# Strassen's scheme for the second projection of four chunks, with attention masks and one FFT side moved to TensorE

## The chip, the cores and the metric

One Trainium2 chip, one core. The metric is device time in microseconds (us) of one execution. The engines are TensorE (PE in the rows; its weight loads are PEld), VectorE (DVE), ScalarE (ACT), GpSimd (POOL) and SyncE (SP), whose queue issues nearly all transfers.

## The reference, cut to what matters

```python
def reference(...):
    x = attention(q, k, v)                   # 8 batches x 8 heads x 576 x 64, heads 0-3 local, 4-7 strided mask
    X = np.fft.fft(np.fft.fft(x, axis=1), axis=2)
    u = x + np.real(X)                       # 8 x 576 x 512
    un = (u - mean) / np.sqrt(var + 1e-6)
    return u + np.maximum(un @ w_ch1, 0.0) @ w_ch2   # 512 x 2048, then 2048 x 512
```

The masks keep for each query the 32 last positions, or the earlier positions of the same residue modulo 32. The weights arrive in double precision and are turned into pairs of 16-bit halves on the chip.

## The kernel before, in words

The 4,608 rows of u make 18 **chunks** of 256 tokens, two for each batch and two extra ones ("x") of leftover rows; the last four chunks are the second of batch 6, the second x chunk and both of batch 7. A chunk runs `ups` (first projection, lines 1316 to 1341), `hidden` (ReLU, 1343 to 1351) and `downs` (second projection, 1353 to 1374). Every product is made from 16-bit halves in three passes (`W3`: high by high, high by low, low by high). For each of 8 steps `fp`, `ups` issues 24 matmuls of 256 columns (line 1333) into a `ph` buffer, ACT makes the ReLU twice (1348, 1349), POOL makes the low half (1351), and `downs` issues 12 matmuls of 512 columns (1372) that add up in the `acc` banks through the whole chunk. `finish` (1376 to 1386) adds the sum to u on DVE (1380), once for each 128 tokens, and stores both.

Ahead of the chunks stand, for each batch, attention over four pairs of heads (`att_first` at 649 for batch 0, `att_pair32` at 566 for batches 1 and 2 in single precision, `att_pair` at 407 for the rest) and the transform (`fft_batch`, 889, with `products32`, 1025, for batch 0). In the single-precision pairs TensorE makes scores (`scores32`, 536), and `weigh` (768) lets DVE scale them, add the mask and write SBUF (777), take the maximum of each block (784) and subtract it (786); ACT then makes one exponential of the whole tile. The transform of batch 0 folds rows on DVE and partly on POOL (894), multiplies on TensorE (A at 1043 and 1045, B at 1066 to 1071, where each of the two sides of a row block is a sum of its own), and DVE adds the input (1075). `norm` (1130) normalises u, splits it in halves (1157, 1160) and transposes them by a DMA (1162) into `uT`, which `ups` reads.

The weights come through a chain of their own: load, two ACT passes (1194, 1196), two DVE passes (1200, 1203), a Gram product on TensorE for a bound on the norm (1227), scales, and the split (1268 ACT, 1270 DVE). The first weight matrix is scaled by quarters, the second only when all 16 of its pieces have gone through the Gram product, so no `downs` can start before that.

The order on each engine is written at build time by a list scheduler (`Order`, 192): every piece of work is an `Op` with an engine, an estimated duration, buffers that it gets and puts back, events that it needs and sets, and a bias from the table `P`; the scheduler takes the operation that can start first, the lower bias among those that lie close. On the chip the engines keep that order and wait on semaphores. Where TensorE would idle in the plan while the first Gram sums are open, `rest` (1231) fills it with matmuls of zeros (1235). PSUM holds two `big` buffers of two banks (scores, transposes, attention outputs, transform), two `ph` banks and two `acc` banks.

## Time and profile before

| | us |
|---|---|
| median of 3 runs | 963.96 (963.33 to 967.6) |
| the profiled execution, own time | 964.85 |
| its span, first to last instruction | 963.1 |
| PE busy in the span | 929.1 (96%) |
| DVE, ACT, POOL busy | 575.0, 448.5, 298.6 |
| mean granted TensorE clock | 0.985 of 2.4 GHz |

A busy engine is one with an instruction in flight; a group's busy time is the union of its instructions, so a mean of a pipelined matmul (274 ns) is longer than its share of the busy time (398.2 us over 3,456, or 115 ns). Times in the rows count from the start of the span.

### The profile page before, as it was taken

Reading aid. Unit: us, or ns where it says so; the run is one execution under the profiler, and the core shown is the slowest. Engines: PE = TensorE matmul, PEld = TensorE weight load, DVE = VectorE, ACT = ScalarE, POOL = GpSimd, SP = SyncE. Lnnn points to the kernel's source line nnn. Section 1 sums busy time; section 2 is a strip of 40 time slices with the busy share of each in tenths; the row PEclk is TensorE's granted clock in tenths of the full one; section 3 lists DMA queues with packets and bytes.
Section 4 is the critical chain, followed back from the end, with each engine's and each line's share of the span. In section 5 each row is a group of like instructions: output and inputs, shape, how many; then the busy total and the mean of one; then the engine's idle time right before and its main releaser. Section 6 shows DMA issues by size and latency. Waiting matters only on the chain.

```text
span 963.1 us, 23556 instructions
## 1 busy us (share of the span) xinstructions
PE 929.1 (96%) x9947; PEld 649.8 (67%) x9947; DVE 575.0 (60%) x1086; ACT 448.5 (47%) x867; POOL 298.6 (31%) x288
## 2 busy tenths in 40 slices
...
GB/s 335 285 262 174 195 131 158 97 67 184 138 35 137 153 51 123 47 194 88 148 31 131 145 143 29 149 138 150 17 80 126 36 12 39 45 1 45 1 22 23
DMA packets 133610, 105.08 MB, mean 109 GB/s; under 512 B 103136, under 2 KB 111744, under 8 KB 133504
## 3 DMA queue, kind: packets, MB, share of 16 engines
...
## 4 chain that ended last, share of the span: by engine, by line
PE 88%; DVE 5%; DMA 3%; issue 1%; ACT 1%; POOL 0%; SPq 0%; DVEq 0%; POOLq 0%; ACTq 0%
PE acc L1372 38%; PE ph L1333 38%; PE B L1021 2%; PE s L485 2%; PE A L998 2%; PE o L516 1%; DMA v<-in_v 1%; DVE W L1200 1%; DMA vlx<-in_v 1%; DMA W<-in_w 1%; PE o L523 1%; DVE W L1203 1%; PE B L1070 1%; PE A L1045 1%; DMA q<-in_qk 1%
## 5 line engine op out<-in xcount | busy, mean ns | idle before, releaser
L1333 PE MATMUL ph<-uT,W 128*128 128x256 f16 x3456 | 398.2, 274 | 1.3 <-issue 0.5
L1372 PE MATMUL acc<-W,h 128*128 128x512 f16 x1728 | 387.1, 379 | 0.0
L1333 PEld LDWEIGHTS <-W 128*128 128x128 f16 x3456 | 334.8, 98 | 56.2 <-issue 6.2
L1351 POOL TENSOR_TENSOR h<-hf,h 128x512 f16<-128x512 f32 x144 | 181.3, 1259 | 462.8 <-ACT h L1349 377.9
L1372 PEld LDWEIGHTS <-h 128*128 128x128 f16 x1728 | 166.2, 98 | 186.3 <-issue 1.2
L1348 ACT ACTIVATE hf<-ph 128x512 f32<-128x512 f32 x144 | 85.6, 594 | 311.8 <-PE ph L1333 285.3
L1349 ACT ACTIVATE h<-ph 128x512 f16<-128x512 f32 x144 | 85.1, 591 | 0.0
L1380 DVE SCALAR_TENSOR_TENSOR u<-acc,cout,u 128x512 f32<-128x512 f32 x32 | 23.6, 745 | 95.5 <-PE acc L1372 95.5
L1141 POOL TENSOR_TENSOR rstd<-mv,negh 128x1 f32<-128x1 f32 x36 | 25.6, 713 | 85.3 <-DVE mv L1138 75.4
L1160 DVE TENSOR_TENSOR unp<-un,unp 128x512 f16<-128x512 f32 x34 | 30.1, 884 | 30.5 <-ACT unp L1157 30.4
L1151 DVE TENSOR_SCALAR un<-u,mv,rstd 128x512 f32<-128x512 f32 x30 | 17.5, 584 | 42.4 <-POOL rstd L1141 40.4
L462 DVE SCALAR_TENSOR_TENSOR kt<-qk,sc,kt 128x576 f16<-128x576 f32 (+1 forms) x40 | 35.6, 930 | 11.1 <-ACT kt L447 10.9
L786 DVE TENSOR_TENSOR sm<-sm,mx 128x864 f32<-128x864 f32 (+1 forms) x32 | 34.5, 1077 | 0.6
L1120 ACT ACTIVATE pq<-B,fcm 128x128 f32<-128x128 f32 (+7 forms) x105 | 27.2, 380 | 15.9 <-PE B L1021 8.4
L447 ACT ACTIVATE kt<-qk,sc 128x576 f16<-128x576 f32 (+1 forms) x40 | 29.3, 783 | 10.7 <-DVE sc L403 6.9
L1011 DVE SCALAR_TENSOR_TENSOR AT<-A,AT 128x290 f16<-128x290 f32 (+3 forms) x35 | 15.1, 480 | 27.1 <-ACT AT L1006 27.1
L894 POOL TENSOR_TENSOR FD<-E 128x381 f32<-128x381 f32 x8 | 10.4, 1299 | 61.4 <-DVE E L894 61.4
L784 DVE TENSOR_REDUCE mx<-sm 128x9 f32<-128x864 f32 (+1 forms) x32 | 29.1, 908 | 0.6
L1110 DVE TENSOR_TENSOR rt<-pq 128x257 f32<-128x257 f32 (+1 forms) x42 | 18.8, 488 | 16.9 <-ACT pq L1120 14.9
L497 ACT ACTIVATE sm<-sm 128x864 f32<-128x864 f32 (+1 forms) x20 | 16.2, 812 | 26.2 <-DVE sm L786 26.2
L1157 ACT CAST unp<-un 128x512 f16<-128x512 f32 x34 | 20.9, 615 | 15.4 <-DVE un L1151 9.4
...
## 6 DMA issues: line engine op xcount, KB each, us to landing
...
```

What stands on the lines that cost most here:

```text
L447: A.activation(hi, src, AF.Copy, scale=f)
L462: V.scalar_tensor_tensor(out=lo, in0=src, scalar=f, in1=hi, op0=ALU.mult, op1=ALU.subtract)
L784: V.tensor_reduce(out=mx[:, 0:nb], in_=sm, axis=AX.X, op=ALU.max)
L786: on(o).tensor_tensor(out=sm, in0=sm, in1=mx[:, 0:nb].rearrange("p (g o) -> p g o", o=1).to_broadcast([128, nb, w]), op=ALU.subtract)
L1120: A.activation(dst, ps[0:r, c0:c1], AF.Copy, scale=cm[0:r])
L1141: G.tensor_tensor(out=rstd, in0=mv[:, 1:2], in1=negh, op=ALU.pow)
L1160: on(o).tensor_tensor(out=unp[:, 1], in0=un, in1=unp[:, 0], op=ALU.subtract)
L1333: T.matmul(ph[:, i, :], W1[:, 4 * (f0 // 512) + d, x, f0 % 512 : f0 % 512 + 128], self.uhl[y][:, d, :], start=(n == 0), stop=(n == 11))
L1348: A.activation(hf, ph, AF.Relu, scale=HS)
L1349: A.activation(hh, ph, AF.Relu, scale=HS)
L1351: G.tensor_tensor(out=hl, in0=hf, in1=hh, op=ALU.subtract)
L1372: T.matmul(self.acc[s], (hh, hl)[x][:, i, 128 * s : 128 * s + 128], W2[:, f, y, :], start=(f == 0 and n == 0), stop=(f == 15 and n == 2))
```

## The change

- **Second projection.** When a chunk above number 2 is about to start its first projection in the plan and table 3 of 8 is made by then, it runs `ups7`, `hidden7`, `downs7`, `finish7` in place of the old path; that holds for the last four chunks. Two halves of the 256 tokens, of the hidden features and of the output columns make a 2 by 2 block product, done with 7 block products in place of 8. `hidden7` builds the sums of hidden blocks (four DVE or POOL operations), ACT and POOL or DVE split seven blocks of 128 columns. `downs7` issues for each fp 21 matmuls of 256 columns, three of the chunk's first 21 being 512 wide, into both `big` buffers. `finish7` combines the sums on ACT and DVE.
- **Tables.** `seven` waits until attention of batch 7 is through and the second matrix is split, gives back the attention's SBUF pools and spawns `combos`, which makes four differences of weight blocks for each fp.
- **Masks.** In single-precision pairs `scores32` opens each PSUM bank with one matmul of the identity by the mask in 16 bits (480 columns local, 324 strided), and the scores add to it. `soft32` takes the maximum from PSUM. For batch 0 DVE subtracts it from PSUM; for batches 1 and 2 (`X1`, `X2` = 1) ACT makes one exponential for each block with the maximum as its bias, 9 or 11 in all, reading PSUM.
- **Batch 0.** `cos2`, `sin2` and both `side` steps are fixed to DVE. B makes both sides of a row block in one bank of 512 columns, and DVE adds them in three operations. For chunk 0 `norm` transposes on TensorE, with ACT and DVE making the halves out of PSUM, without the DMA.
- **Small things.** The norm bound of a quarter is one DVE operation in place of three; a table of the transform is split in two loads; pools change sides; every number of `P` that steers the order is new.

```diff
         w, per = (WIN, 5) if local else (GR, NG2)
         off = [(g // per) * 512 + (g % per) * w for g in range(nb)]
+        one = ident.bitcast(BF16).rearrange("p (n t) -> p n t", t=2)[:, :, 1]
+        if local:
+            m = mloc.rearrange("p g w -> p (g w)").bitcast(BF16).rearrange("p (g w t) -> p g w t", g=5, t=2)[:, :, :, 1]
+            masks = m, m[:, 1:2].to_broadcast([128, per, w])
+        else:
+            m = mstr.bitcast(BF16).rearrange("p (o w t) -> p o w t", o=1, t=2)[:, :, 0:w, 1]
+            masks = (m.to_broadcast([128, per, w]),) * 2
                 for h in range(2):
                     hs = slice(64 * h, 64 * h + 64)
-                    T.matmul(ps[rows(local, g, h), off[g] : off[g] + w], qk[hs, st : st + 64], qk[hs, S + st : S + st + w], start=True, stop=True)
+                    T.matmul(ps[rows(local, g, h), off[g] : off[g] + w], qk[hs, st : st + 64], qk[hs, S + st : S + st + w], start=False, stop=g in (per - 1, nb - 1))
         return w, off
...
+    def soft32(nm, ps, local, sm, out, split, note, get, put, room, also, sets=""):
+        nb, per, w = (NQB, 5, WIN) if local else (NG, NG2, GR)
+        yield op("V", (1.15 if local else 0.82) + (0.1 if split else 0.0), put=also, note=f"max {nm}")
+        mx = small.tile([128, 2 * NG2], F32, tag="mx", name=f"my{nm}_{room}")
+        src = ps.rearrange("p (b c) -> p b c", b=2)[:, :, 0 : per * w].rearrange("p b (g w) -> p b g w", w=w)
+        V.tensor_reduce(out=mx[:, 0 : 2 * per].rearrange("p (b g) -> p b g", b=2), in_=src, axis=AX.X, op=ALU.max)
+        if split:
+            V.tensor_scalar(mx[:, 0 : 2 * per], mx[:, 0 : 2 * per], -0.125, None, op0=ALU.mult)
+            yield op("A", 2.7 if local else 2.8, get=get, put=f"{put} {room}", sets=sets, note=f"exp {nm}")
+            for g in range(nb):
+                A.activation(out[:, g], src[:, g // per, g % per], AF.Exp, scale=0.125, bias=mx[:, g : g + 1])
+            return
+        yield op("V", 1.25 if local else 0.82, put=room, note=f"sub {nm}")
+        if local:
+            for b, n in ((0, 5), (1, 4)):
+                m = mx[:, 5 * b : 5 * b + n].rearrange("p (g o) -> p g o", o=1).to_broadcast([128, n, w])
+                V.tensor_tensor(out=sm[:, 5 * b : 5 * b + n], in0=src[:, b, 0:n], in1=m, op=ALU.subtract)
+        else:
+            m = mx.rearrange("p (b g o) -> p b g o", b=2, o=1).to_broadcast([128, 2, per, w])
+            V.tensor_tensor(out=sm.rearrange("p (b g) w -> p b g w", b=2), in0=src, in1=m, op=ALU.subtract)
+        yield op("A", 0.92 if local else 0.7, get=get, put=put, sets=sets, note=f"exp {nm}")
+        A.activation(out, sm[:, 0:nb], AF.Exp, scale=0.125)
...
         def side(c0, c1, nm, sd):
-            o = op("V", 0.75 if c0 else 1.4, need=(f"sin{b}" if c0 else nm) if f32 else nm, sets=f"FH{c0}_{b}" if f32 else "", note=f"SD{c0} {b}", alt=dict(G=(1.5, P["LSD"])))
+            o = op("V", 0.75, need=(f"sin{b}" if c0 else nm) if f32 else nm, sets=f"FH{c0}_{b}" if f32 else "", note=f"SD{c0} {b}", alt=None if f32 else dict(G=(1.5, P["LSD"])))
...
-            ps = psbig(f"B{b}_{t}")
-            for i in range(2):
-                R = ps[:, 512 * i : 512 * i + 257]
-                T.matmul(R, zerb, zero.to_broadcast([128, 257]), start=True, stop=False)
-                for g, (c0, w) in enumerate(GROUPS):
-                    k0, k1, st = cols[g]
-                    tc0 = c0 if i or g < 3 else c0 + 255
-                    T.matmul(R[0:r, k0:k1:st], AT[0:w, g, 128 * t : 128 * t + r], tb[0:w, tc0 : tc0 + w], start=False, stop=False)
-                T.matmul(R, zerb, zero.to_broadcast([128, 257]), start=False, stop=True)
-            spawn(sums(b, t, r, xa, xb, ps[0:r, 0:257], ps[0:r, 512:769], "big"), bias=P["t2"] if t == 2 else None)
+            yield op("T", 2.5, get="big" + (" u" if t < 2 else ""), need=" ".join(f"AT{g}_{b}" for g in range(5)), put="f6" if t == 2 else "", sets="!b1" if t == 1 else "", note=f"B{t} {b}")
+            R = psbig(f"B{b}_{t}")[:, 0:512]
+            T.matmul(R, zerb, zero.to_broadcast([128, 512]), start=True, stop=False)
+            c = 0
+            for g, (c0, w) in enumerate(GROUPS):
+                lhs = AT[0:w, g, 128 * t : 128 * t + r]
+                st, k0 = steps[0][g], steps[1][g]
+                if g == 0:
+                    T.matmul(R[0:r, 0:257:4], lhs, tb[0:w, 0:65], start=False, stop=False)
+                    T.matmul(R[0:r, 260:512:4], lhs, tb[0:w, 65:128], start=False, stop=False)
+                    c = 128
+                else:
+                    o = R[0:r].rearrange("p (i k) -> p i k", i=2)[:, :, k0:256:st]
+                    T.matmul(o, lhs, tb[0:w, c : c + 2 * w].rearrange("p (i k) -> p i k", i=2), start=False, stop=False)
+                    c += 2 * w
+            T.matmul(R, zerb, zero.to_broadcast([128, 512]), start=False, stop=True)
+            spawn(sums32(b, t, r, xa, xb, R[0:r]), bias=P["t2"] if t == 2 else None)
...
+    def sums32(b, t, r, xa, xb, R):
+        for i in range(2):
+            yield op("V", 0.68 if i == 0 else 0.75, put="big" if i else "", need="xk0" if i else "", sets=("", (f"u{b}a0", f"u{b}a1", "")[t])[i], note=f"u{t} {b}")
+            if i == 0:
+                if t < 2:
+                    uu = mp.tile([128, 2, DM], F32, tag="u", name=f"u{b}_{t}", bufs=UB)
+                    dst = [uu[:, 0], uu[:, 1]]
+                else:
+                    dst = [xa[0:33, 2], xb[0:33, 2]]
+                V.tensor_tensor(out=dst[0], in0=R, in1=xa[0:r, t], op=ALU.add)
+            else:
+                V.tensor_tensor(out=dst[1][:, 1:512], in0=R[:, 511:0:-1], in1=xb[0:r, t, 1:512], op=ALU.add)
+                V.tensor_tensor(out=dst[1][:, 0:1], in0=R[:, 0:1], in1=xb[0:r, t, 0:1], op=ALU.add)
+        yield from placed(b, t, dst, xa, xb)
...
@@ -1149,6 +1207,18 @@
         else:
             un = mp.tile([128, 2, 257], F32, tag=tag, name=f"un{nm}", bufs=P["RB"]).rearrange("p a b -> p (a b)")[:, 0:DM]
         V.tensor_scalar(un, u, mv[:, 0:1], rstd, op0=ALU.subtract, op1=ALU.mult)
+        if c == 0:
+            yield op("T", 0.95, get="big", put=tag, note=f"uT {nm}")
+            ps = psbig(f"uT{nm}")[:, 0:512]
+            for d in range(4):
+                T.transpose(ps[:, 128 * d : 128 * d + 128], un[:, 128 * d : 128 * d + 128], ident)
+            ps = ps.rearrange("p (d t) -> p d t", d=4)
+            hi, lo = uT[:, 0:4, 128 * s : 128 * s + 128], uT[:, 4:8, 128 * s : 128 * s + 128]
+            yield op("A", 0.65, note=f"uhi {nm}")
+            A.copy(hi, ps)
+            yield op("V", 0.68, put="big", sets=f"uT{nm}", note=f"ulo {nm}")
+            V.tensor_tensor(out=lo, in0=ps, in1=hi, op=ALU.subtract)
...
+    def seven():
+        yield op("S", 0, need=" ".join([f"xd{B - 1}_{hp}" for hp in range(4)] + [f"w1_{m}" for m in range(8)]), note="seven")
+        early.close()
+        late_["p"] = ctx.enter_context(tc.tile_pool(name="late", bufs=1, side="right", reuse_waits="tile"))
+        S_.room["x"] = [S_.now] * 2
+        S_.room["hq"] = [S_.now] * 2
+        yield op("G", 0.5, sets="t2_z", note="zeros")
+        TT[0] = late_["p"].tile([128, 2, 5, 256], F16, name="T0")
+        G.memset(W2[:, 16, 0, 0:256], 0.0)
+        G.memset(TT[0][:, 0, 4], 0.0)
+        for fp in range(8):
+            spawn(combos(fp), bias=P["T"] + 0.1 * fp)
...
+    def combos(fp):
+        o = op("V", 1.15, get="x x", note=f"tr {fp}", alt=dict(G=(2.6, P["LT"])))
+        yield o
+        R = xt(f"tr{fp}").rearrange("p (k a) c -> p k (a c)", k=2)
+        W = W2[:, 2 * fp : 2 * fp + 2]
+        on(o).tensor_tensor(out=R, in0=W[:, :, 0], in1=W[:, :, 1], op=ALU.add)
+        o = op("V", 1.4, note=f"ts {fp}", alt=dict(G=(2.8, P["LT"])))
+        yield o
+        X = xt(f"ts{fp}").rearrange("p (k a) c -> p k (a c)", k=4)
+        b11, b12, b21, b22 = R[:, 1, 0:256], R[:, 1, 256:512], R[:, 0, 0:256], R[:, 0, 256:512]
+        for k, x, y in ((0, b12, b11), (1, b22, X[:, 0]), (2, b22, b12), (3, b21, X[:, 1])):
+            on(o).tensor_tensor(out=X[:, k], in0=x, in1=y, op=ALU.subtract)
+        yield op("A", 1.0, note=f"thi {fp}")
+        if fp:
+            TT[fp] = late_["p"].tile([128, 2, 4, 256], F16, name=f"T{fp}")
+        A.copy(TT[fp][:, 0, 0:4], X)
+        o = op("V", 1.15, put="x x", sets=f"t2_{fp}", note=f"tlo {fp}", alt=dict(G=(2.6, P["LT"])))
+        yield o
+        on(o).tensor_tensor(out=TT[fp][:, 1, 0:4], in0=X, in1=TT[fp][:, 0, 0:4], op=ALU.subtract)
     HS = 2.0**-14
...
         def ups(self):
             c = self.c
+            self.seven = False
+            if c > 2:
+                yield op("T", 0, need=f"uT{c}_0 uT{c}_1 up{c - 1}", note=f"up {c}")
+                self.seven = S_.events.get(f"t2_{P['TQ']}", 1e9) < S_.now
+            spawn(self.downs7() if self.seven else self.downs(), bias=P["dn"])
+            if self.seven:
+                yield from self.ups7()
+                return
             for fp in range(8):
...
+        def hidden7(self, fp, ph):
+            c = self.c
+            yield op("A", 0.62, get="x", put="ph", note=f"relu {c} {fp}")
+            X = xt(f"x{c}_{fp}")
+            A.activation(X[:, 4:8].rearrange("p k t -> p (k t)"), ph, AF.Relu, scale=HS / 2)
+            o = op("V", 0.85, note=f"hsum {c} {fp}", alt=dict(G=(1.7, P["LX"])))
+            yield o
+            for k, x, y, f in ((0, 7, 5, ALU.add), (1, 0, 6, ALU.subtract), (2, 6, 7, ALU.subtract), (3, 4, 1, ALU.subtract)):
+                on(o).tensor_tensor(out=X[:, k], in0=X[:, x], in1=X[:, y], op=f)
+            yield op("A", 0.9, note=f"hhi {c} {fp}")
+            if fp % 2:
+                h = f6(f"h{c}_{fp}").bitcast(F16)[:, 0:1792].rearrange("p (y k t) -> p y k t", y=2, k=7)
+            else:
+                h = late_["p"].tile([128, 2, 7, 128], F16, tag="hq", name=f"h{c}_{fp}", bufs=2)
+            self.h[fp] = h
+            A.copy(h[:, 0], X[:, 0:7])
+            o = op("G", 2.3, put="x", sets=f"h{c}_{fp}", note=f"hlo {c} {fp}", alt=dict(V=(0.98, P["LH"])))
+            yield o
...
+        def downs7(self):
+            c = self.c
+            for fp in range(8):
+                first, last = fp == 0, fp == 7
+                yield op("T", 2.32, get="big big" if first else "", put="f6" if fp % 2 else "hq", need=f"h{c}_{fp} t2_{fp} t2_z" + (f" down{c - 1}" if first else ""), sets=f"down{c}" if last else "", at=0, note=f"down {c} {fp}", slack=0.3)
+                if first:
+                    self.pa, self.pb = psbig(f"pa{c}"), psbig(f"pb{c}")
+                h, t = self.h.pop(fp), TT[fp]
+                w = lambda k, half: lambda y: W2[:, 2 * fp + k, y, 256 * half : 256 * half + 256]
+                tt = lambda k: lambda y: t[:, y, k]
+                wide = {0: W2[:, 1:17:15, 0, 0:256], 2: W2[:, 0:17:16, 0, 0:256], 4: TT[0][:, 0, 2:5:2]}
+                for k, (ps, q, x, m) in enumerate((
+                    (self.pa, 0, 6, w(1, 0)), (self.pa, 1, 1, tt(1)), (self.pa, 2, 4, w(0, 0)), (self.pa, 3, 0, tt(0)),
+                    (self.pb, 0, 2, tt(2)), (self.pb, 1, 5, tt(3)), (self.pb, 2, 3, w(0, 1)),
+                )):
+                    for n, (y, z) in enumerate(W3):
+                        if first and n == 0 and k in wide:
+                            T.matmul(ps[:, 256 * q : 256 * q + 512].rearrange("p (a t) -> p a t", a=2), h[:, y, x], wide[k], start=True, stop=False)
+                        else:
+                            T.matmul(ps[:, 256 * q : 256 * q + 256], h[:, y, x], m(z), start=first and n == 0 and k == 6, stop=last and n == 2 and (k % 2 == 1 or k == 6))
+            spawn(self.finish7(), bias=P["ev"])
...
+        def finish7(self):
+            c, pa, pb = self.c, self.pa, self.pb
+            e = yield op("A", 1.05, get="x", note=f"ev {c}")
+            ev = xt(f"ev{c}").rearrange("p (k a) t -> p k (a t)", k=4)
+            A.activation(ev, pa.rearrange("p (k t) -> p k t", k=4), AF.Copy, scale=cout2)
+            yield op("V", 1.7, put="big", at=e - 0.9, note=f"fin {c}")
+            stt = lambda out, ps, x: V.scalar_tensor_tensor(out=out, in0=ps, scalar=cout2, in1=x, op0=ALU.mult, op1=ALU.add)
+            add = lambda e, out, x, y: e.tensor_tensor(out=out, in0=x, in1=y, op=ALU.add)
+            stt(self.u[0][:, 256:512], pb[:, 512:768], self.u[0][:, 256:512])
+            stt(self.u[1][:, 0:256], pb[:, 256:512], self.u[1][:, 0:256])
+            add(V, ev[:, 1], ev[:, 1], ev[:, 0])
+            u0 = self.u[0].rearrange("p (k t) -> p k t", k=2)
+            u1 = self.u[1].rearrange("p (k t) -> p k t", k=2)
+            add(V, u0, u0, ev[:, 0:2])
+            yield op("V", 0.4, put="big", note=f"fin7 {c}")
+            stt(ev[:, 1], pb[:, 0:256], ev[:, 1])
+            o = op("V", 1.2, note=f"fin7 {c}", alt=dict(G=(2.4, P["LF"])))
+            yield o
+            add(on(o), u0, u0, ev[:, 2:4])
+            add(on(o), u1, u1, ev[:, 1:2].to_broadcast([128, 2, 256]))
+            o = op("V", 0.35, put="x", note=f"fin7 {c}", alt=dict(G=(0.7, P["LF"])))
+            yield o
+            add(on(o), self.u[1][:, 256:512], self.u[1][:, 256:512], ev[:, 3])
+            yield from self.store()
...
@@ -1449,10 +1661,11 @@
     for b in range(1, B):
         spawn(batch(b), bias=1 + 0.1 * b)
+    S_.room["x"], S_.room["hq"] = [], []
+    spawn(seven(), bias=0)
     for ch in chunks:
         spawn(ch.norm(), bias=P["p0"] if ch.c == 0 else P["p1"] if ch.c == 1 else P["pn"])
         spawn(ch.ups(), bias=P["up"])
```

## Rows read from the trace of the kernel before

**Rows 1.** The page: busy us of each engine, share of the span, instructions.
```profile
PE 929.1 (96%) x9947; PEld 649.8 (67%) x9947; DVE 575.0 (60%) x1086; ACT 448.5 (47%) x867; POOL 298.6 (31%) x288
```
**Rows 2.** The page: chain that ended last, shares of the span.
```profile
PE 88%; DVE 5%; DMA 3%; issue 1%; ACT 1%; POOL 0%; SPq 0%; DVEq 0%; POOLq 0%; ACTq 0%
```
**Rows 3.** Windows: length, PE, PEld, DVE, ACT, POOL busy (instructions), clock, DMA share, GB/s.
```profile
0.00:88.00 88.00, 69.03 (x899) 55.73 (x900) 68.88 (x121) 51.56 (x75) 12.28 (x14) 0.88 0.81 273
88.00:146.00 58.00, 51.82 (x754) 44.30 (x753) 48.87 (x92) 31.90 (x56) 14.98 (x13) 0.95 0.58 163
146.00:192.00 46.00, 45.85 (x470) 28.42 (x470) 34.02 (x56) 22.66 (x39) 14.74 (x14) 1.00 0.42 129
192.00:740.00 548.00, 543.84 (x6290) 374.12 (x6288) 375.17 (x733) 286.90 (x584) 196.45 (x192) 1.00 0.44 107
740.00:797.00 57.00, 57.00 (x440) 39.44 (x439) 27.41 (x53) 20.43 (x50) 22.75 (x21) 1.00 0.18 50
797.00:964.00 167.00, 161.51 (x1105) 107.83 (x1102) 20.65 (x34) 35.08 (x65) 37.44 (x35) 0.99 0.09 25
```
**Rows 4.** Windows, line 1235 alone (zero matmuls): length, PE and PEld busy, clock, DMA.
```profile
0.00:88.00 88.00, 24.85 (x347) 23.65 (x347) 0.88 0.81 273
```
**Rows 5.** Chain in order of time, last chunk: start, length, what.
```profile
942.91 5.24 PE ph L1333 x48
948.15 10.37 PE acc L1372 x48
```
**Rows 6.** Timeline of the end: start, length, engine, line, what.
```profile
958.03 1.63 SPq L1386 DMA_DIRECT2D out<-u  x2
958.55 0.75 DVE L1380 SCALAR_TENSOR_TENSOR u<-acc,cout,u 128x512 f32<-128x512 f32 x1 [0.55 <-PE acc L1372]
```
**Rows 7.** Lines by form, DVE and ACT: prices near the new operations.
```profile
L1075 DVE TENSOR_TENSOR u<-rt,xa 128x257 f32<-128x257 f32 x14 | 5.9, 420 | 0.0
...
L870 ACT COPY xb<-xb0a 128x1024 f32<-128x1024 f32 x1 | 1.0, 1012 | 1.0 <-DVE O L894 1.0
```
**Rows 8.** Lines, DVE, 0 to 146 us: the mask, the subtraction.
```profile
L786 DVE TENSOR_TENSOR sm<-sm,mx 128x864 f32<-128x864 f32 (+1 forms) x8 | 8.0, 1006 | 0.2
...
L777 DVE SCALAR_TENSOR_TENSOR sm<-s,mloc 128x480 f32<-128x480 f32 (+1 forms) x10 | 5.6, 599 | 6.6 <-PE s L544 6.6
...
L777 DVE SCALAR_TENSOR_TENSOR sm<-s,mstr 128x324 f32<-128x324 f32 (+1 forms) x8 | 3.3, 458 | 1.0 <-PE s L544 1.0
```
**Rows 9.** Timeline, DVE: a fold; the split alone and beside POOL.
```profile
34.65 2.48 DVE L1270 SCALAR_TENSOR_TENSOR W<-W,scl,W 128x1024 f16<-128x1024 f32 x2 [1.21 <-ACT W L1268]
...
50.10 0.56 DVE L894 TENSOR_TENSOR FD<-E 128x381 f32<-128x381 f32 x1
50.58 3.97 DVE L1270 SCALAR_TENSOR_TENSOR W<-W,scl,W 128x1024 f16<-128x1024 f32 x2
```
**Rows 10.** Timeline, POOL: the folds of batch 0.
```profile
51.48 1.98 POOL L894 TENSOR_TENSOR FD<-tmp 128x384 f32<-128x384 f32 x1
53.54 2.73 POOL L894 TENSOR_TENSOR E<-FD 128x257 f32<-128x257 f32 x2
```
**Rows 11.** Timeline, PE and SP: first product A, uT's transposes, first `ups`.
```profile
56.33 0.75 PE L1045 MATMUL A<-f32a,E 128*65 128x145 f32 x2 [0.67 <-POOL E L894]
...
80.42 3.50 SPq L1162 DMA_TRANSPOSE uT<-unp  x2
...
87.56 0.61 PE L1227 MATMUL gram<-W 128*128 128x128 bf16 x4 [2.80 <-DVE W L1203]
87.96 6.64 PE L1333 MATMUL ph<-uT,W 128*128 128x256 f16 x48
```
**Rows 12.** Line 1351 (POOL, low half): shortest, median, longest ns; first and last start.
```profile
L1351 POOL TENSOR_TENSOR h<-hf,h x144: 1146/1158/2876, 93.3 to 949.5; 128x512 f16<-128x512 f32 x144
```
**Rows 13.** Line 1120 by form (ACT, one block with a pointer scale).
```profile
L1120 ACT ACTIVATE pq<-B,fcm 128x65 f32<-128x65 f32 x14 | 5.3, 378 | 11.3 <-PE B L1021 7.5 <-DVE rt L1110 3.8
```

152 lines of the change are left out of this document (90 added, 62 removed).

## The prediction

> **What bounds the kernel now.** I read the page's busy line first: TensorE is busy for 96% of the span, no other engine over 60% [rows 1]. The chain of waits says the same: 88% of it is TensorE, 5% VectorE, 3% DMA [rows 2]. An average hides the stages, so the table of stretches comes next [rows 3]. From 192 us on TensorE stands still for 4 us in 605 until the last stretch, whose 5.5 us are the end of the kernel; there only TensorE work counts. Until 88 us it is another picture: TensorE shows 69.0 us busy, but 24.9 of these are matmuls of zeros [rows 4], so with the 19.0 idle ones half of the stretch does nothing for the result, while DVE is busy for 68.9. From 88 to 146 us DVE has 48.9 of 58 and TensorE idles 6.2: this is the second weight matrix being prepared, and the first `downs` waits for its end. So the front is set by DVE and the loads, and all behind 146 us by TensorE.
>
> The last chunk gives the price of both projections [rows 5]: 48 matmuls of 256 columns in 5.24 us, 109.2 ns each; 48 of 512 columns in 10.37 us, 216.0 ns each. A chunk's `downs` is 96 of these, 20.74 us.
>
> **Strassen, TensorE.** A new `downs7` is 8 x 21 = 168 matmuls, of which 3 are 512 wide. Taking the 256-column price from `ups`, which also has one weight load for each matmul, it costs 165 x 0.1092 + 3 x 0.2160 = 18.67 us, 2.07 less than before. Four chunks: **-8.3 us**. Bounds: nothing gained if each block waits for its data; -9.1 if the price were half that of 512 columns (165 x 0.1080 + 0.65 = 18.47, 2.27 a chunk). I take -8.3, since the row is of the same shape.
>
> The rule that speaks against this is in the Trainium skill, "TensorE: Matmul & The Clock Gate", section "Back-to-back issue gap": in a stream of pairs of weight load and matmul it gives about 131 ns for 512 columns and 81 for 128, as weight loads share the spacing. By that rule 96 old matmuls would cost 12.6 us and 168 new ones, at some 98 ns by interpolation (an estimate from that page), 16.4, so each chunk would lose 3.8 and the four 15 us in place of the gain of 8.3. The trace here disagrees with the 131 ns: 216.0 [rows 5].
>
> **Work beside it.** For each fp, ACT makes one ReLU and one copy of 7 x 128 = 896 columns where it made two of 512; by 1.01 us for 1,024 columns [rows 7] that is some 1.5 us of a step of 2.62 + 2.33 = 4.95 us. POOL's low half grows from 1.16 us at 512 columns [rows 12] to 2.03 at 896, and four block sums of 128 columns on DVE are under 4 x 0.42 [rows 7]. All stay below the step. Every hidden step holds one of two new `x` buffers from its ReLU to its low half: 0.6 + 1.0 + 0.9 + 2.0, with hand-overs some 5 us; two buffers carry one step each 2.5 us. The tables cost DVE and POOL 8 times two operations of 1,024 columns and four of 256; by 257 columns in 0.42 us that is 8 x 5 = 40 us, and ACT 8 x 1.0. They are spread over the two stretches behind attention, where DVE has 29.6 of 57 us free before the last four chunks begin at 797 us [rows 3], and POOL takes part. Price: nothing; without that cover the first new chunk would simply take the old path, 2.07 us each. `downs7` takes both `big` buffers, but the transform of batch 7 has ended by then.
>
> **The end.** Now one DVE operation of 0.75 us follows the last matmul, then the store [rows 6]. After the change two 256-column additions wait for the last matmul, then come 256, 512, 256, 512, 512 and 256 columns in turn on DVE, ACT's copy of 1,024 columns (1.01 us) running beside. With 0.42 us for 257 columns [rows 7] and 0.75 for 512 [rows 6], and some tenths off where neighbours overlap (an estimate), this is 5 x 0.37 + 3 x 0.60 = 3.65 us: **+2.9 us**. Bounds: +3.6 without overlap, +5 with an addition on POOL, +2 if sums from PSUM start ahead of the last matmul.
>
> **Masks.** One local pair gets two matmuls of 480 columns, a strided one two of 324: 2 x 0.203 and 2 x 0.138 us by the prices above, 1.36 us for the four pairs of a batch. In batch 0 they fall into a stretch half of which is zeros or idle, in batch 1 into 88 to 146 us: both at nothing, hidden by DVE's chain; 1.4 us each if that cover is gone. Batch 2 runs on the saturated engine: **+1.4 us**. The scores now need mask and identity loaded, some tenths of loading ahead of the first scores, and one more table load goes through SP's queue, behind which the weights wait; both are inside the front's bounds.
>
> **The front.** DVE loses the mask step of eight pairs by 146 us: 5.6 us for ten instructions and 3.3 for eight, of which eight and eight go, 7.8 us [rows 8]. In batch 1 the subtraction goes too, half of 8.0 [rows 8], 4.0; four small scalings come, 0.6. Fixing `cos2`, `sin2` and two sides on DVE adds 2 x 0.56 [rows 9] and 2 x 0.84 [rows 7], 2.8. But POOL then leaves it alone: the split took 3.97 us beside POOL and 2.48 alone [rows 9], -1.5. Sum: 9.9 us less DVE work ahead of the first `downs`. Batch 0's 3.9 us of masks lie in the first 24 us, where loads decide, so 6.0 are left. The same is seen along the chain to the first `ups`: A starts at 56.33 behind POOL's folds of 1.98 and 2.73 us [rows 10, 11]; on DVE, from 50.66 on, the two take 1.4, so A starts 4.2 us earlier. B in one bank saves some, and the transposes of 3.5 us in SP's queue [rows 11] go to TensorE, ACT and DVE. The first `ups` at 87.96 stood behind a Gram product that waited 2.8 us for DVE [rows 11]; the next gate is the second matrix. I take **-6 us**, between 0 (loads or staging buffers of the second matrix decide) and -12 (all 9.9 and a shorter Gram wait). For batches 1 and 2 ACT makes 9 or 11 exponentials in place of one; with 0.38 us for the first of five small ones [rows 13], overlapping, 2.5 to 4 us for each pair, hidden while ACT has 26 of 58 us free. The scores' PSUM buffer is held for that long instead of 1.2 us.
>
> **Sum.** -8.3 + 2.9 + 1.4 - 6.0 = -10.0 us against the profiled execution's own 964.85: 954.9. That execution stands 0.9 us above the median of the three runs, so against these **954.0 us** (-1.0%). This measurement can tell about 0.5%, 4.8 us.
>
> **Rivals.**
> - *The front gives nothing.* The second matrix comes in its 16 loads through staging buffers, at a DMA share of 0.58 [rows 3]; if these set the first `downs`, DVE's gain is idle time. Against: DVE is busy 84% there. 960.0 us, no change that can be told. Chance 0.22.
> - *The front gives double*, as the zero matmuls and idle time leave 44 us to be had before 88 us: 947 us. Chance 0.14.
> - *It does not do what it says*: tables or `big` buffers come so late that two chunks' gain is lost, +4: 958. Chance 0.06; free DVE time speaks against it.
> - *The hidden chain becomes the bound* (the other side). DVE's sums and POOL's low half hinder each other: line 1351's median is 1.16 us, its longest 2.88 [rows 12]. The `x` buffer is held 5 us; this decides from 9.9 us on, twice the step. At 11 us a step takes 5.5 in place of 4.95: 32 steps x 0.55 = +17.6 us, 972 us. Chance 0.08: most executions of the row are at the median. The Trainium skill, "GPSIMD Engine Reference", section "8. Key points", says that POOL shares its SBUF interfaces with VectorE's operations of two SBUF inputs, which the new sums are; the trace agrees [rows 9].
> - *Weight loads show.* A load takes 107.83 / 1,102 = 0.098 us [rows 3]. If it were not hidden behind 256 columns of the new pattern, 168 x 0.207 = 34.8 us replace 20.74: +56 in place of -8.3, 1,018 us. `ups` hides it, so chance 0.02. The page's rule above goes the same way; by its figures the time would be some 978.
>
> **How the numbers follow.** The forecast has 0.48, its own range 949 to 959. Faster: 0.48 + 0.14 + 0.06 = 0.68. Same: 0.22. Slower: 0.08 + 0.02 = 0.10. The range leaves out the slower cases and the far end of the double front: 944 to 964.
>
> **What would show it.** In the changed profile: 21 matmuls in about 2.33 us in the last four chunks and TensorE at 100% there; one DVE train of some 3.7 us after the last matmul; first A near 52 us, first `ups` near 80, first `downs` near 140; no more than 5 us of idle TensorE behind 192 us. The forecast is wrong if `downs7` waits on its hidden blocks, if the first `downs` stays at 146 us, or if TensorE waits for `big` buffers in batches 1 and 2.

## The result, and the profile after

The changed kernel takes **957.15 us** (median of 5 runs, 954.85 to 958.69) where the kernel before took 964.67 beside it (5 runs, 963.33 to 967.8): a ratio of 0.9904 [0.9875, 0.9932]. The forecast was 954.0 with 944 to 964. The profiled execution took 954.85 us, 10.0 less than the profiled one before; the forecast's sum was -10.0. So the number came out, but two of its parts did not, and they cancel.

The page first: busy time by engine, and the chain that ended last (against [rows 1, 2]).

```profile
PE 921.2 (97%) x10190; PEld 675.1 (71%) x10190; DVE 664.0 (70%) x1296; ACT 485.8 (51%) x951; POOL 263.5 (28%) x252
...
PE 88%; DMA 4%; DVE 4%; issue 1%; ACT 1%; SPq 1%; ACTq 0%; DVEq 0%
```

TensorE still sets the time; DVE has 89 us more to do, and its part of the chain is 4%, after 5% before. The table of stretches, cut at the new milestones (first `ups` at 82 us, first `downs` at 134), columns as in [rows 3]:

```profile
0.00:82.00 82.00, 65.58 (x840) 50.56 (x841) 58.73 (x110) 46.66 (x68) 3.73 (x8) 0.91 0.79 273
82.00:134.00 52.00, 51.23 (x760) 44.12 (x759) 44.79 (x86) 41.74 (x98) 15.77 (x13) 0.98 0.67 202
134.00:192.00 58.00, 57.83 (x614) 36.87 (x605) 38.32 (x72) 35.50 (x96) 16.07 (x18) 1.00 0.43 129
192.00:797.00 605.00, 598.03 (x6647) 412.00 (x6645) 441.13 (x838) 313.10 (x627) 225.37 (x210) 0.99 0.41 100
```

Ahead of 134 us TensorE idles 17 us in place of 25 ahead of 146. Behind 192 it idles 7.0 us, where 4.2 stood before and at most 5 were forecast.

To see where each kernel gains and loses I took from each trace the start of the first `ups` (first matmul of `ph`), of the first `downs`, and of the `ups` of chunks 2, 3 and 13 in TensorE's order (the 385th, 577th and 2,497th matmul of `ph`). "Rest" is from chunk 13's start to the end of TensorE's last matmul, and "tail" from there to the end of the span. All in us; the kernels below the second line are the experiments.

| kernel | ups | downs | chunk 2 | chunk 3 | chunk 13 | rest | tail |
|---|---|---|---|---|---|---|---|
| before | 88.0 | 146.1 | 214.6 | 254.9 | 739.05 | 219.46 | 4.6 |
| changed | 81.9 | 134.2 | 208.8 | 248.6 | 734.32 | 211.22 | 7.5 |
| changed_again | 83.7 | 136.1 | 210.1 | 250.0 | 733.14 | 211.22 | 7.5 |
| no_strassen | 83.1 | 135.5 | 209.6 | 248.4 | 732.76 | 219.45 | 4.2 |
| masks_on_dve | 83.7 | 137.4 | 210.3 | 248.1 | 731.75 | 215.58 | 7.5 |
| folds_on_pool | 89.5 | 141.1 | 214.7 | 253.9 | 739.73 | 213.91 | 7.5 |
| gather_held | 83.7 | 134.8 | 210.4 | 249.0 | 731.81 | 211.44 | 8.0 |
| order_alone | 101.4 | 159.8 | 242.3 | 288.8 | 762.46 | 219.46 | 4.6 |
| chunk_2_turned_on_tensore | 82.5 | 134.3 | 205.0 | 242.9 | 725.77 | 211.22 | 7.2 |
| last_chunk_old | 86.6 | 137.8 | 211.9 | 250.7 | 731.35 | 217.64 | 4.5 |
| turned_no_strassen | 85.1 | 137.0 | 207.4 | 245.3 | 726.43 | 219.46 | 3.8 |
| turned_last_old | 82.8 | 133.5 | 204.5 | 242.5 | 723.77 | 213.28 | 4.2 |
| turned_last_old_gather_held | 84.0 | 135.8 | 206.2 | 248.1 | 738.37 | 213.28 | 4.1 |
| chunk_0_by_transfer | 89.8 | 143.0 | 216.7 | 253.9 | 734.58 | 211.22 | 7.5 |

The first two lines are the whole result: 4.7 us of lead at chunk 13, 8.24 less in the rest, 3.0 more in the tail, -10.0 in all.

How far a single line can be trusted, four of them tell: changed, changed_again, no_strassen and last_chunk_old run the same order on TensorE, DVE and ACT up to 700 us, and their first `downs` come at 134.2 to 137.8, their chunk 13 at 731.4 to 734.3. So a start is known to some 3 us. Lengths between two starts repeat better, from the first `downs` to chunk 2 for instance 74.0 to 74.6 in these four, and most readings below are such lengths.

The lead over the kernel before was 11.9 us at the first `downs`. It is half gone by chunk 2; in the other three of the four it is 8.3 to 10.6 and 2.7 to 5.0. The timeline of TensorE ahead of chunk 2, and the second of chunk 2's two transposes in SP's queue, in the changed kernel; then two stretches of it (columns as above):

```profile
203.43 1.26 SPq L1232 DMA_TRANSPOSE uT<-unp  x1
...
208.77 4.45 PE L1455 MATMUL ph<-uT,W 128*128 128x256 f16 x20 [2.06 <-DMA uT<-unp]
```
```profile
204.00:209.00 5.00, 1.84 (x58) 1.11 (x57) 3.91 (x9) 0.94 (x1) 4.06 (x5) 0.83 0.86 221
209.00:216.00 7.00, 7.00 (x43) 5.31 (x42) 2.86 (x5) 1.59 (x3) 1.95 (x5) 0.63 0.95 337
```

TensorE is busy 1.84 of 5 us: it has nothing left but a few scores, waits 2.06 us at the end for chunk 2's transposes, which are used 5.3 us after their issue, and then works at a mean granted clock of 0.63 for 7 us, that is, for most of them at the lower level, 1.2 GHz. The kernel before issued the same transposes at 208.48 and used them at 214.56, 6.1 us later, but there work lay between. Its timeline of TensorE (line 631 is attention's product, 1372 `downs`):

```profile
209.10 1.27 PE L631 MATMUL o<-vlx,pT 96*64 96x65 f32 x36
210.30 0.88 PE L620 MATMUL t<-ident,pbt 128*128 128x128 f32 x6
211.02 2.75 PE L1372 MATMUL acc<-W,h 128*128 128x512 f16 x12
213.70 0.93 PE L563 MATMUL o<-vsx,pT 54*64 54x65 f32 x48
214.56 1.70 PE L1333 MATMUL ph<-uT,W 128*128 128x256 f16 x14
```

### The profile page after: what moved, and what is told of

Same layout as the page of the kernel before. It is cut to its first block, busy times and chain, and to the rows that moved or that the text cites. A ratio compares the mean times of both kernels' runs of the same rounds, so it can differ in the third digit from the quotient of the medians.

```text
span 953.1 us, 24270 instructions
## 1 busy us (share of the span) xinstructions
PE 921.2 (97%) x10190; PEld 675.1 (71%) x10190; DVE 664.0 (70%) x1296; ACT 485.8 (51%) x951; POOL 263.5 (28%) x252
## 4 chain that ended last, share of the span: by engine, by line
PE 88%; DMA 4%; DVE 4%; issue 1%; ACT 1%; SPq 1%; ACTq 0%; DVEq 0%
PE ph L1455 30%; PE acc L1581 30%; PE ph L1472 9%; PE pa L1524 4%; PE pb L1524 3%; PE B L1054 2%; PE s L500 2%; PE A L1031 1%; DMA q<-in_qk 1%; PE o L531 1%; DMA vn<-in_vl 1%; PE s L568 1%; PE o L538 1%; DMA vlx<-in_v 1%; DMA W<-in_w 1%
## 5 line engine op out<-in xcount | busy, mean ns | idle before, releaser
L1581 PE MATMUL acc<-W,h 128*128 128x512 f16 x1344 | 302.6, 379 | 0.0
L1560 POOL TENSOR_TENSOR h<-hf,h 128x512 f16<-128x512 f32 x112 | 149.3, 1333 | 334.6 <-ACT h L1558 262.4
L1581 PEld LDWEIGHTS <-h 128*128 128x128 f16 x1344 | 128.7, 98 | 142.7 <-issue 0.5
L1557 ACT ACTIVATE hf<-ph 128x512 f32<-128x512 f32 x112 | 66.8, 596 | 178.6 <-PE ph L1455 134.6
L1524 PEld LDWEIGHTS <-h 128*128 128x128 f16 x660 | 64.6, 98 | 8.9
L1491 DVE TENSOR_TENSOR x<-x 128x128 f32<-128x128 f32 x128 | 31.5, 287 | 43.3 <-ACT x L1487 42.2
L1501 DVE TENSOR_TENSOR h<-x,h 128x896 f16<-128x896 f32 x32 | 34.9, 1092 | 25.0 <-ACT h L1498 24.9
L1498 ACT CAST h<-x 128x896 f16<-128x896 f32 x32 | 30.0, 939 | 42.1 <-DVE x L1491 40.4
L1487 ACT ACTIVATE x<-ph 128x512 f32<-128x512 f32 x32 | 19.1, 597 | 60.1 <-PE ph L1472 60.1
L1524 PE MATMUL pa<-T,h 128*128 128x256 f16 x192 | 31.4, 273 | 0.0
L1524 PE MATMUL pa<-W,h 128*128 128x256 f16 x184 | 30.5, 273 | 0.0
```

The costliest lines, as they stand in the source:

```text
L1491: on(o).tensor_tensor(out=X[:, k], in0=X[:, x], in1=X[:, y], op=f)
L1498: A.copy(h[:, 0], X[:, 0:7])
L1501: on(o).tensor_tensor(out=h[:, 1], in0=X[:, 0:7], in1=h[:, 0], op=ALU.subtract)
L1524: T.matmul(ps[:, 256 * q : 256 * q + 256], h[:, y, x], m(z), start=first and n == 0 and k == 6, stop=last and n == 2 and (k % 2 == 1 or k ...
L1557: A.activation(hf, ph, AF.Relu, scale=HS)
L1560: G.tensor_tensor(out=hl, in0=hf, in1=hh, op=ALU.subtract)
```

## The experiments

They ran in three sets, each on one chip: the first four below (kernel before: 964.67 us, median of 25 runs, from 959.67 to 973.56), the next four (961.46, 11 runs), the last four (958.85, 24 runs). With that spread, medians of different sets say nothing within 3 us; what is compared is the ratio to the runs of before beside them, and the table above.

**No Strassen.** The scheme is left out with its tables, so all chunks use the old second projection.
```diff
-    spawn(seven(), bias=0)
-                self.seven = S_.events.get(f"t2_{P['TQ']}", 1e9) < S_.now
+                self.seven = False
```


> All 18 chunks take the old second projection and no tables are built; all else, and the order up to the tables, is that of the changed kernel. If the four Strassen chunks give back 2.07 us each on TensorE and cost 2.9 us at the end, as the trace of the changed kernel reads (8.2 less, 3.0 more), this runs some 5 us above the changed kernel: about 962 us, its last matmul 8 us later, 4.65 us from there to the end. Rival: the new hidden chain or the tables already ate the gain elsewhere (DVE work for tables beside the last old chunks); then it runs within 2 us of the changed kernel, about 957.

957.92 us (12 runs, 954.45 to 962.63), 0.9928 [0.9899, 0.9957]. The medians differ by 0.8 us and the ratios by 2.3, less than expected; but the rest is 219.45 against 211.22, and the tail 4.2 against 7.5. By the trace the scheme is worth 8.2 - 3.3 = 4.9 us, and this execution came to chunk 13 1.6 us earlier, which the scheme doesn't explain: changed_again, below, has the scheme and comes there within 0.4 us of it. The times left it open (962 was expected); turned_no_strassen, below, settles it.

**Masks on DVE again.** Order held.
```diff
-            T.matmul(ps[...], one, m, start=True, stop=False)
+            V.scalar_tensor_tensor(out=sm[:, g0:g1], in0=src[...], scalar=1.0, in1=m, op0=ALU.mult, op1=ALU.add)
```


> The masks go back to DVE (the same order of work, one mask step from PSUM to SBUF ahead of each maximum; blocks of exponentials then read SBUF), and the 24 mask matmuls are gone. If DVE sets the front, the first second-projection matmul moves from 134.2 us to about 138 (the 3.9 us of batch 1's four mask steps; batch 0's lie in the shadow of the loads) and the end by 4 less 1.4 of TensorE in batch 2: about 2.5 us slower than the changed kernel, 959.5. Rival: the lead of the front came from the new order alone; then the first such matmul stays at 134 and the kernel is 1 to 3 us faster, about 955.

958.12 us (8 runs), 0.9942 [0.9919, 0.9966]. First `downs` at 137.39, where about 138 was expected. From the first `ups` to the first `downs` it takes 53.7 us, against 51.1 to 52.4 in changed, changed_again, no_strassen, gather_held and last_chunk_old: the masks' place is worth 1.3 us or more there, with TensorE waiting 2.1 us for DVE in the Gram products, where the changed kernel shows none. Chunk 13 starts 1.4 us earlier than in changed_again, not later: batch 2's masks are off TensorE, no wait at chunk 2 is over 0.5 us (several small ones are left), and no lower clock follows. The profiled execution then loses 2.5 us at 749, where TensorE waits for DVE (told at last_chunk_old). So in this execution nothing of the masks' gain is left at chunk 13; the medians leave it open.

**Folds on POOL again** (`cos2`, `sin2` and both sides of batch 0; order held).
```diff
-                tt_(on(o), sd[:, t], FD[:, 0, c0:c1], FD[:, 1, c0:c1], f)
+                tt_(on(o) if b else G, sd[:, t], FD[:, 0, c0:c1], FD[:, 1, c0:c1], f)
```


> The four last folds of batch 0 go back from DVE to POOL, with the order of all engines as in the changed kernel. If these folds are on the way to the first chunk, the first product A starts some 3 us later (POOL took 1.98 and 2.73 us where DVE takes 0.55 and 0.76), the first chunk's first projection by 3, and the first second projection by 1 to 3: end 1 to 3 us later, 958 to 960. Rival: the second weight matrix is the next gate whatever chunk 0 does; then the first second projection stays at 134.2 and the end at 957.

960.48 us (12 runs), 0.9954 [0.9926, 0.9982]. The timeline of POOL and of TensorE:
```profile
56.74 3.36 POOL L927 TENSOR_TENSOR O<-FD 128x255 f32<-128x255 f32 x2
60.06 1.40 POOL L927 TENSOR_TENSOR E<-FD 128x257 f32<-128x257 f32 x2
...
60.83 1.43 PE L1078 MATMUL A<-f32a,E 128*65 128x145 f32 x4 [6.68 <-POOL E L927]
```
In the changed kernel DVE makes them in a fraction, and A starts at 55.01:
```profile
53.87 0.75 DVE L927 TENSOR_TENSOR O<-FD 128x255 f32<-128x255 f32 x2
54.53 0.76 DVE L927 TENSOR_TENSOR E<-FD 128x257 f32<-128x257 f32 x2
...
55.01 0.80 PE L1078 MATMUL A<-f32a,E 128*65 128x145 f32 x4 [1.81 <-DVE E L927]
```
First `ups` and `downs` come 5.8 and 5.0 us later than in changed_again, more than the 3 and the 1 to 3 expected. So the new order leans on DVE's folds. But this is not what they brought against the kernel before, where POOL made them and started them earlier; its first product A on `E` stands only 0.2 us behind the changed kernel's:
```profile
55.19 0.46 PE L1045 MATMUL A<-f32a,E 128*65 128x145 f32 x2 [2.17 <-POOL E L894]
```

**Gather held.** Batch 2's load of its first rows may be ordered only behind chunk 2's transposes, so that it doesn't share the DMA engines with them.
```diff
-... need=" ".join(f"xd{b}_{hp}" for hp in range(4)), note=f"xa {b}")
+... need=" ".join(f"xd{b}_{hp}" for hp in range(4)) + (" uT2_0 uT2_1" if b == 2 else ""), note=f"xa {b}")
```


> In the changed kernel TensorE idles 2.1 us at 206.7 us for the transposed halves of chunk 2, while the loads of batch 2's rows (direct and gathered) fill the DMA engines, and then shows a granted clock of 0.58 for the next stretch of 5 us. Here these loads wait until chunk 2's transposes are through. If the transposes were late because of these transfers, the idle time and the half clock go: 4 to 5 us faster than the changed kernel, about 952.5. Rival: the transposes are late for themselves, or the later loads make batch 2 late instead; then the idle time only moves, and the time stays within 1.5 us of 957.

952.99 us (5 runs), 0.9883 [0.9857, 0.9908], the 952.5 expected, but by luck, not for the reason given. TensorE's wait for the transposes is no shorter:
```profile
203.87 1.26 SPq L1232 DMA_TRANSPOSE uT<-unp  x1
...
206.05 0.39 SPq L912 DMA_DIRECT2D xa<-xd  x1
...
210.42 2.96 PE L1455 MATMUL ph<-uT,W 128*128 128x256 f16 x13 [2.98 <-DMA uT<-unp]
```
The load (912) still goes out before the transposes have landed, 2.2 us behind their issue where it was 1.8 in the changed kernel, so the edit did not part the two; whether the load delays them is not answered. Up to 210 us the order on TensorE, DVE and ACT is the changed kernel's; behind that the edit moved it, and chunk 13 starts 1.3 us earlier than in changed_again. What lowers the time stays open; by the ratios it is 2 us, inside the intervals.

**The changed kernel once more.** No edit.

> The changed kernel once more, with no edit, so that the runs beside it are compared on one chip. Theory: the 2.1 us wait of chunk 2's `ups` for the transposes' transfer at 207 us, and the half clock behind it, belong to the order of the work, so they are there again: over 1.5 us of wait, 3.4 to 6.8 us at the lower clock between 200 and 220 us, and about 957 us. Rival: they were an accident of one execution; then the wait is under 0.5 us and the profiled time about 952.

954.09 us (6 runs), 0.9908 [0.9873, 0.9943]. The wait is there again, 2.83 us, with the lower clock behind it; no_strassen has 2.42 and last_chunk_old 2.90. It belongs to the order.

**The order alone.** The kernel before with the changed kernel's numbers in `P`.

> The kernel before with the new numbers of the order and none of the new code. Theory: the numbers were fitted to other parts and are worth nothing without them: 962 to 972 us, first `downs` no sooner than 143 us, where the changed kernel has 134. Rival: the order alone made the shorter front; then first `ups` stand at about 82 us, first `downs` at about 134 to 138, and the time is 957 to 960 with the Strassen steps' 5.2 us missing.

987.96 us (6 runs), 1.0263 [1.0224, 1.0301]: worse than the theory's 962 to 972. The two longest waits of TensorE (us, times, longest):
```profile
PE gram L1228 <- DVE W L1204: 7.2, 3, 5.1
PE ph L1334 <- DMA uT<-unp: 7.2, 2, 6.8
```
The numbers are a fit to durations that the old code doesn't have: the first `downs` moves to 159.8, and chunk 2's transposes are bare for 6.8 us, with no head start at all. The gain is the new parts' and the order's together, and none of it the order's alone.

**Chunk 2 turned on TensorE**, as chunk 0 is.
```diff
-        if c == 0:
+        if c in (0, 2):
             yield op("T", 0.95, get="big", put=tag, note=f"uT {nm}")
```


> Chunk 2's rows are transposed on TensorE as chunk 0's are, eight transposes more and no transfer. Theory: what was lost at 204 to 215 us is the transfer's own 5 to 6.5 us from issue to use, which nothing covered, and the half clock after it: 2.1 us idle and 1.7 to 3.4 us by the clock go, and 1.4 us of transposes come (four start within 0.4 us in the front), so 2 to 4 us less than the changed kernel on the same chip, about 954, and no half clock between 190 and 240. Rival: TensorE had no other work there whatever chunk 2 does (attention of batch 2 is late); then a wait of about the same length stands at the next line and the time is the changed kernel's or 1.4 us more.

**944.07 us** (6 runs, 938.32 to 948.7), **0.981** [0.977, 0.9849]: 10 us less than the changed kernel on the same chip (7.5 between the two profiled executions), more than the 2 to 4 expected. TensorE's timeline, and the same 12 us in both kernels (first this one, then changed_again):
```profile
201.91 0.60 PE L1214 MATMUL uT<-ident,un 128*128 128x128 f32 x4
202.35 0.17 PE L375 MATMUL n<-ss,oneb 128*128 128x3 bf16 x1
202.38 2.75 PE L1581 MATMUL acc<-W,h 128*128 128x512 f16 x12
204.96 2.78 PE L1455 MATMUL ph<-uT,W 128*128 128x256 f16 x24
```
```profile
204.00:216.00 12.00, 12.00 (x154) 10.12 (x152) 11.73 (x20) 5.86 (x10) 8.22 (x10) 1.00 1.06 279
```
```profile
204.00:216.00 12.00, 8.84 (x93) 5.70 (x91) 8.02 (x18) 3.12 (x5) 5.72 (x8) 0.72 0.88 268
```
TensorE goes from `downs` into `ups` with no gap and at 2.4 GHz throughout (1.00 against 0.72). Chunk 3 starts 7.1 us earlier than in changed_again and chunk 13 7.4; of these 1.8 were there at the first `downs`, ahead of anything that the edit moves, so 5.6 are its own. The lead of 11.8 us at the first `downs` stands at 13.3 at chunk 13. That is the cause of the give-back, shown: a transfer that the new order leaves without cover, with the lower clock behind the wait. From the first `downs` to chunk 2 all eight kernels that have the new order and this transfer take 72.9 to 75.6 us, the four with chunk 2 turned 70.4 to 71.0, the kernel before 68.4. That TensorE comes earlier is not what bares it, as chunk_0_by_transfer shows.

**The last chunk the old way.**
```diff
-                self.seven = S_.events.get(f"t2_{P['TQ']}", 1e9) < S_.now
+                self.seven = S_.events.get(f"t2_{P['TQ']}", 1e9) < S_.now and c < 17
```


> The last of the four chunks does its second projection the old way; the three before it keep the Strassen steps. Theory: the end costs what the trace of the changed kernel shows, 7.6 us from TensorE's last matmul to the end against 4.65 before, so about 2.9 us come back and 2.07 us of TensorE are lost again: 0.8 us less than the changed kernel on the same chip. Rival: the longer end is the output transfers' own, whatever DVE does: the tail stays at about 7 us and the time is 2 us more.

951.08 us (6 runs, 947.27 to 955.35), 0.9879 [0.9842, 0.9917], 3.0 us less than changed_again where 0.8 was expected, with intervals that overlap. The tail is 4.5 us, as the theory had it: the longer end is DVE's train, not the stores'. The profiled execution (955.35) has a loss of its own in the rest. Timeline, DVE and TensorE:
```profile
746.04 1.22 DVE L1399 TENSOR_TENSOR ts<-tr 128x256 f32<-128x256 f32 x1
...
747.29 0.83 DVE L1399 TENSOR_TENSOR ts<-tr,ts 128x256 f32<-128x256 f32 x1
748.04 0.94 DVE L1399 TENSOR_TENSOR ts<-tr 128x256 f32<-128x256 f32 x1
...
748.90 1.37 DVE L1399 TENSOR_TENSOR ts<-tr,ts 128x256 f32<-128x256 f32 x1
750.19 0.74 DVE L1589 SCALAR_TENSOR_TENSOR u<-acc,cout,u 128x512 f32<-128x512 f32 x1
...
750.98 5.30 PE L1581 MATMUL acc<-W,h 128*128 128x512 f16 x16 [2.52 <-DVE u L1589]
```
Line 1399 builds the Strassen tables. Four of its differences stand in DVE's order ahead of a chunk's final sum (1589), which frees the `acc` bank that TensorE needs. Where POOL works beside them they take 0.83 to 1.37 us, and TensorE waits 2.5 us; with what the clock loses behind it (0.91 from 745 to 765 us) the rest is 4.4 longer than in turned_last_old. In the changed kernel's own trace, two of the four ran alone and TensorE did not wait:
```profile
748.29 0.43 DVE L1399 TENSOR_TENSOR ts<-tr,ts 128x256 f32<-128x256 f32 x1
748.63 0.42 DVE L1399 TENSOR_TENSOR ts<-tr 128x256 f32<-128x256 f32 x1
```
There the four take 2.9 us from the first's start to the last's end, here 4.2, so POOL explains 1.3 of the 2.5. The other part: in this execution TensorE started chunk 13 3.0 us earlier, and DVE the first of the four only 1.0. masks_on_dve and folds_on_pool have the same 2.5 us. So the tables are free only while the cover is there, to a microsecond or two.

**Chunk 2 turned, no Strassen.** The edits of these two runs together.

> Chunk 2 turned on TensorE, and all four last chunks by the old second projection. Theory: on this quieter base Strassen is worth what the trace of the changed kernel shows, 8.2 us less TensorE and 3.0 us more behind the last matmul, so this is 5.2 us longer than the kernel with chunk 2 turned and Strassen kept (0.981 of before): 0.986 of before, and 6 us longer than the run beside it that keeps three Strassen chunks. Rival: as the first try without Strassen read (957.92 beside 957.15), the scheme is worth about 1 us, because its table building and its busier VectorE cost elsewhere what TensorE saves: 0.982.

951.80 us (7 runs), 0.992 [0.9889, 0.995], where 0.986 was expected. Against turned_last_old beside it, 7.3 us more, where 6 were expected. The table divides the profiled difference of 8.4: 2.7 were there at chunk 13, 6.18 come in the rest, which is three chunks of 2.06, and 0.4 goes in the tail. Against chunk_2_turned_on_tensore the table gives 8.2 more in the rest and 3.4 less in the tail, 4.9 for four chunks. The rival, a scheme worth 1 us, falls.

**Chunk 2 turned, the last chunk old.** Two of the edits above together.

> Chunk 2 turned on TensorE, the last chunk's second projection the old way, the three before it by Strassen. Theory: TensorE 2.07 us longer and the tail 3.0 us shorter than with chunk 2 turned alone: 0.9 us less, 0.980 of before, about 943; from the last matmul to the end 4.5 us. Rival: the tail stays over 6 us and the time is 946.

944.46 us (4 runs, 943.38 to 944.84), 0.9849 [0.9815, 0.9883]. The rest is 2.06 longer and the tail 2.9 shorter than with chunk 2 turned alone. The net, 0.9 us less, is as expected and too small for the times to show; the ratio, expected at 0.980, stands above that kernel's 0.981, inside the intervals. This one has the shortest profiled span of all (941.3).

**The same with the gather held.** The edit of gather_held on top.

> As the run beside it, and the planner may order batch 2's load of its first rows only behind chunk 2's transposes. Theory: with no transfer of transposes left to be late, holding the load gives nothing, or delays batch 2's transform by a microsecond: 0 to 2 us more than the run beside it. Rival: what the held load gained before (952.99 beside 957.15) was not the wait but a better order of the middle; then 2 to 4 us less, about 940.

953.06 us (12 runs, 946.91 to 959.16), 0.9925 [0.9891, 0.9959]: 8.6 more than the run beside it, which neither side expected. The edit moved the order of the middle, and in the profiled execution (957.67) attention's transpose by DMA is now bare ahead of 622.6 us:
```profile
PE o L531 <- DMA pT<-qk: 5.6, 1, 5.6
```
The same small edit came with less time in one order and more in another.

**Chunk 0 by transfer.** Its transposes as DMAs again, the halves made on ACT and DVE.
```diff
-                T.transpose(ps[:, 128 * d : 128 * d + 128], un[:, 128 * d : 128 * d + 128], ident)
+            nc.sync.dma_start_transpose(uT[:, :, 128 * s : 128 * s + 128], unp.rearrange("p x d -> p (x d)"))
```


> The changed kernel with chunk 0's transposes as transfers again, as the kernel before had them. Theory: the front's head start is the shorter chain ahead of the first `ups`, of which the transfer is 3.5 us where the transposes on TensorE, the copy and the subtract are 2 us; the first `ups` move from 82 to 84 to 86 us and the first `downs` by as much, but first `downs` wait for the filter weights and the sums more than for `ups`, so the time rises by 0 to 3 us on the same chip, 0.991 to 0.994 of before. Rival: TensorE's idle time grows by the whole transfer under load, 5 to 6.5 us as chunk 2's took, and the half clock behind it: 0.997 or more.

956.68 us (12 runs), 0.9969 [0.9945, 0.9992], by the ratio the rival's 0.997. But the trace shows the theory's 2 to 4 us: the second transpose is issued at 86.70, and TensorE waits 2.96 us for it. The first `ups` and `downs` come 6.1 and 6.9 us later than in changed_again, and of these 2.9 were there at the first product B (71.97 against 69.10), ahead of the edit. From B to the first `ups` it takes 17.9 us against 14.6, so the transfer costs 3.3. (The 3.50 us of [rows 11] are SP's queue issuing two of them, not the time to their use.)
```profile
86.70 1.25 SPq L1217 DMA_TRANSPOSE uT<-unp  x1
...
89.84 5.30 PE L1452 MATMUL ph<-uT,W 128*128 128x256 f16 x24 [2.96 <-DMA uT<-unp]
```
At chunk 13 only 1.4 us are left. By the ratios it costs some 6 us, by the profiled times (955.04 against 953.66) 1.4; between these it stays open. And this run tells what bares chunk 2's transposes. The order is the changed kernel's; of the head start 3.1 us are left at the first `downs`, the second transpose is issued at 212.76, 4.3 us later than in the kernel before, and TensorE waits for it all the same:
```profile
212.76 1.27 SPq L1229 DMA_TRANSPOSE uT<-unp  x1
...
216.71 2.56 PE L1452 MATMUL ph<-uT,W 128*128 128x256 f16 x22 [2.02 <-DMA uT<-unp]
```
```profile
217.00:224.00 7.00, 7.00 (x66) 6.26 (x65) 5.90 (x8) 3.22 (x6) 3.64 (x7) 1.00 1.03 360
```
So it is what the order puts between issue and use, a few scores, and not how early TensorE comes; order_alone, with no head start, agrees. Here the clock stayed at its upper level behind the wait, and the stretch from the first `downs` to chunk 13 is 591.5 us, against 597.0 in changed_again.

## Why the prediction was right, and where it was not

**Strassen, -8.3: right.** The rest shrinks by 8.24 us, and every pair of kernels that differs in the scheme, and has no wait of its own there, gives 2.06 for each chunk. A step of `downs7` in the last chunk, its first two groups of matmuls, its last, and the first of the next step:
```profile
936.21 0.49 PE L1524 MATMUL pa<-W,h 128*128 128x256 f16 x3
936.53 0.49 PE L1524 MATMUL pa<-T,h 128*128 128x256 f16 x3
...
938.17 0.49 PE L1524 MATMUL pb<-W,h 128*128 128x256 f16 x3
938.50 0.49 PE L1524 MATMUL pa<-W,h 128*128 128x256 f16 x3
```
It takes 2.29 us: 21 matmuls at 109 ns, the price of `ups`. The Trainium skill, "TensorE: Matmul & The Clock Gate", section "Back-to-back issue gap", gives 131 ns for 512 columns in a stream of weight loads and matmuls; the trace disagrees, 216.0 ns [rows 5]. The loss that the prediction estimates from that page did not come, and 256 columns take 109 ns where its estimate has some 98. Weight loads don't show, and the hidden chain is no bound: from 797 us to the last matmul TensorE is busy for all of 148.54 us. The prediction gave the low halves to POOL; there DVE makes them (line 1501, 1.09 us each), and POOL is busy for 2.5 us.

**The end, +2.9: right.** +3.0. DVE's train behind the last matmul:
```profile
945.58 0.88 DVE L1533 SCALAR_TENSOR_TENSOR u<-pb,cout,u 128x256 f32<-128x256 f32 x2 [4.90 <-PE pb L1524]
946.37 0.42 DVE L1534 TENSOR_TENSOR ev<-ev 128x256 f32<-128x256 f32 x1
946.82 0.69 DVE L1534 TENSOR_TENSOR u<-u,ev 128x512 f32<-128x512 f32 x1
947.55 0.48 DVE L1533 SCALAR_TENSOR_TENSOR ev<-pb,cout,ev 128x256 f32<-128x256 f32 x1
947.95 1.74 DVE L1534 TENSOR_TENSOR u<-u,ev 128x512 f32<-128x512 f32 x3
```
It is 4.1 us long, 945.58 to 949.69, against 3.65 worked out. The last chunk alone earns 2.06 and pays 3.0.

**The front, -6: inside its range, but not by the steps named.** At the first `downs` the lead is 11.9 us, the end of the range ("-12, all 9.9 and a shorter Gram wait"), and 8.3 to 10.6 in three more executions of the same order. The step that the prediction drew along the chain failed: A's folds were to start A 4.2 us earlier and brought 0.2, 55.01 against 55.19; the 56.33 of [rows 11] is the second half of that product. By the first product B the lead is 1.9 (67.40 against 69.32), by the first `ups` 6.0, at the first `downs` 11.9. Of the 4.1 between B and the first `ups` chunk 0's transposes are 3.3, by chunk_0_by_transfer; the prediction named them without a price. Between the first `ups` and the first `downs` TensorE idled 6.2 us before [rows 3] and idles 0.8 now; of the 5.9 gained there the masks are 1.3 or more, by masks_on_dve. What B in one bank, the exponentials by blocks and the new order bring was not undone one at a time, so some 7 us of the lead are located, but not put down to a part; order_alone shows only that the order without the parts brings none of it. That the lead goes by the sum of DVE's work, 6.0, was not shown. The signs were off with it: A at 55.01, where 52 was forecast, and yet the first `downs` at 134, where it was 140.

**What was left out: +7 between the first `downs` and chunk 13.** "No more than 5 us of idle TensorE behind 192 us" failed at 7.0. From the first `downs` to chunk 13 TensorE idles 2.9 us more than in the kernel before; the lower clock costs 2.6, by (1 - 0.63) x 7 in the stretch shown; the other 1.7 is work. That is batch 2's masks in the main, forecast at +1.4: in the stretch from 134 to 192 us six of their matmuls keep TensorE busy for 1.54. The prediction asked what each removed wait would uncover in the front and stopped at the first `downs`; it did not ask what its new order leaves between chunk 2's transposes and their use. That this transfer and the lower clock behind it carry most of the rest is shown by chunk_2_turned_on_tensore, where none of the lead is lost. How much is lost differs by execution, 7.2, 4.1, 4.3 and 0.6 us in the four of the same order: up to chunk 2 it is 5.6 to 6.1 in all of them, behind it the clock and later waits fall out differently. So -11.9 and +7 stood in for -6 and +1.4, and their sum, -4.7 against -4.6, was right by luck.

**The tables, nothing: right in this execution, thin in others.** The cover named, DVE's 29.6 free microseconds, is an average over a stretch; what counts is when TensorE and DVE come to the same place inside it, and three experiments lose 2.5 us there, in an order that is the changed kernel's at that place.

**The rivals.** "The front gives double" (947 us; by the prediction's own terms 954.0 - 6 is 948.0) describes this execution up to 134 us, and with chunk 2 turned the whole kernel: 0.981 of 964.85 is 946.5. That nothing would come of the front is refuted by the table, but an uncovered transfer came halfway to it: at chunk 2 half the lead was gone.
